# Loads that wait for an instruction instead of a copy, in an attention and expert kernel of one core

## The chip, the cores and the metric

The kernel runs on one core of a Trainium2 chip. The core has a matrix engine (TensorE, "PE" in the profile, with its weight loads shown apart as "PEld"), a vector engine (VectorE, "DVE"), a scalar engine (ScalarE, "ACT"), a general engine (GpSimd, "POOL") and an engine that mostly issues transfers (SyncE, "SP"). Each engine works through its own instructions in order and waits on semaphores for the others; 16 DMA engines move data between the memory outside (HBM) and the one on the core (SBUF). Sums of matrix products are collected in a third memory, PSUM, which has eight banks of 512 numbers per partition.

The metric is device time in microseconds for one execution. Two kernels are compared by the median of several runs of each.

## What is computed

An attention over 8 batches, 8 heads, 576 positions and 64 numbers per head, whose scores get a bias that falls with a running sum of `s`, and behind it a layer of 8 experts, where each token either picks its own expert or keeps that of the token before it:

```python
scores = scale * q @ k.T                                  # causal
cum = cumsum(maximum(s, 0))
attn = softmax(scores - (cum[query] - cum[key]))
x = attn @ v                                              # (8, 576, 512)
logits = x @ w_gate
e = argmax(logits) if s == 0 or sigmoid(x @ w_local) < 0.5 else previous e
out = softmax(logits)[e] * (relu(x @ w1[e]) @ w2[e])
```

Everything is in 32-bit floats. The bias is not added to the scores: the kernel multiplies each value row by exp(cum) of its key ("weighing"), and divides at the end by the sum of the same weights, which it gets from an extra column.

## The kernel before

The order of the instructions on every engine is written out by hand: an engine runs its instructions in the order in which the program names them. A tile of SBUF or PSUM comes from a pool with a fixed number of buffers; whoever first writes a reused buffer waits until its earlier readers are done.

**The attention** works on 32 pairs of heads (four pairs per batch), two pairs in each of 16 *slots*; `m` counts slots, `n` pairs. In a slot TensorE first makes the scores of the slot's two pairs in three units each (`scores`, L903 to L923, matmuls at L916), then half blocks of the diagonal (`scores_halves`, L938, for the next slot, and `values_halves`, L987, for this one), then the weighted sums of the first pair, "po", and of the second, "pb" (`values`, L975). ScalarE turns each unit of scores into exponentials (tile `e`, L917), GpSimd masks the diagonal (L900), VectorE divides (`evacuate`, reciprocal into `recs` and multiply, L997). Scores and the pairs' "pb" sums share three double banks of PSUM in turn (`banks`).

**The weighing** (`weigh`, L885 to L893): a copy on ScalarE (L890) writes the weights' column and two multiplications on VectorE (L893) write the value rows, all into one of four `vg` tiles. It needs the table `wk` of key weights, which is made once, in slot 0: exponentials of the running sum on ScalarE (L857, L858), seven transposes on TensorE (L866) and nine copies on VectorE (L872). `WEIGHED` gives the last pair weighed by the end of each slot.

**The loads** of keys (`kb`), queries (`qb`) and values (`va`) are issued by SP, in order: 288 KB for `kb` and `qb`, 320 KB for `va`. The first four pairs' loads stand at the start. Pair 0's queries and keys come in two parts each so that the first scores can begin early (L807). Later loads are spread over the slots. A slot has named places: `e00` to `e21`, behind each exponential (first digit the unit, second the pair of the slot), `h` behind the half blocks, `x0`, `x1` behind the first pair's two divisions, `y0`, `y1` behind the second's; `POINTS` says which places a slot uses, and `parts_of` gives the loads in order. To keep a load from starting before its place, the program writes one element of the target tile with a copy on ScalarE from something made at that place (L815 for values, L1064 for queries and keys, L548 for weights), so that the load has to wait for the copy:

```python
nc.scalar.copy(to[0:1, 0:1], behind)
nc.sync.dma_start(to, (q, k)["qk".index(what)][b][:, hp])
```

**Other work of the slots** is put at numbered places by `plan(slot, place, f)`: places 0 and 1 behind the two pairs' scores, 3 and 4 behind the first and second pair's divisions, 5 at the end. Among it are the router's products (L222, `lp`), its ranks (L307, L308), and scatters of the result into a table in HBM by GpSimd (L355), most of them in slots 7 to 15. Four loads of 512 KB each, the quarters of the first expert's first weights, are at place 3 of slots 11, 12, 13 and 13.

**The experts** (`Experts.run`) follow: 23 units of tokens, first layer (L614, L605), ReLU on ScalarE (L616), second layer (L643), a scatter to the output (L647). The second weights of the first expert are loaded behind the first ReLU of unit 0, with such a copy (L548); the router's last product also stands in unit 0.

Of the kernel before, what the change touches and what calls it, by code (L numbers as in the profile page):

```python
# [48 lines left out]
XW = 4 * 32 + 2  # L49
NV = 4  # L50
NVA = 6
WEIGHED = (3, 7, 9, 11, 11, 13, 15, 19, 19, 21, 23, 27, 27, 30, 31, 31)
STORES = (((5,), (0, 1, 3, 4, 5), (0, 1, 3, 4, 5), (0, 1, 3, 4, 5), (0, 0)), ((5, 5), (0, 1, 3, 4, 5), (0, 1, 3, 4, 5), (0, 1, 1, 3, 4, 5)),
          ((5, 5), (0, 0, 1, 1, 3, 4, 5, 5)))
BX = 3
FIRST = 3 * P
POINTS = {0: ("h", "x0", "x1", "y0"), 1: ("e00", "e10", "e20", "e01", "e11", "h", "x0", "x1"), 2: ("e00", "e20", "e11", "h", "x0", "x1")}
CAP = N + DH
ROWS = E * CAP + 2 * P
EMPTY = 1 << 20  # L60
# [10 lines left out]
@with_exitstack  # L71
def kernel(
    ctx: ExitStack,
    tc: tile.TileContext,
    q: bass.AP,
    k: bass.AP,
    v: bass.AP,
    s: bass.AP,
    w_gate: bass.AP,
    w_local: bass.AP,  # L80
    wx: bass.AP,
    w1: bass.AP,
    w2: bass.AP,
    out: bass.AP,
):
    nc = tc.nc
    table = nc.dram_tensor("table", (ROWS, 4, XW), F32, kind="Internal")

    ctx.enter_context(tc.manual_schedule(engines=None))
    const = ctx.enter_context(tc.tile_pool(name="const", bufs=1))  # L90
    ident = const.tile([P, P], F32, name="ident")
    make_identity(nc, ident)
    recs = const.tile([P, NPAIR, NJ, 2], F32, name="recs")
    wend = const.tile([P, NPAIR * NJ], F32, name="wend")
    out_of = const.tile([P, 1], I32, name="out_of")

    with ExitStack() as main:
        router = Router(main, tc, ident, table)
        experts = Experts(main, tc, w1, w2, out, table, router)
        with ExitStack() as early:  # L100
            attention(early, tc, q, k, v, s, wx, ident, recs, wend, router, experts)
        experts.run(recs, wend, out_of)

    wrong = nc.values_load(out_of[0:1, 0:1], min_val=0, max_val=1 << 23,
                           skip_runtime_bounds_check_because="a count of elements and rows")
    with tc.If(wrong > 0):
        cum_d = nc.dram_tensor("cum", (B * H, S), F32, kind="Internal")
        x_d = nc.dram_tensor("x_tokens", (N, D), F32, kind="Internal")
        with tc.tile_pool(name="g_const", bufs=1) as g:
            lg = g.tile([P, NM, E + 1], F32, name="lg")  # L110
            nc.vector.memset(lg, 0.0)
            ebi = g.tile([P, NBLK], I32, name="ebi")
            idx_g = g.tile([P, NBLK], I32, name="idx_g")
            idx_s = g.tile([P, NBLK], I32, name="idx_s")
            gate = g.tile([P, NBLK], F32, name="gate")
            attention_general(tc, q, k, v, s, w_gate, w_local, cum_d, x_d, ident, lg)
            route(tc, ident, lg, ebi, idx_g, idx_s, gate)
            experts_general(tc, w1, w2, out, x_d, ident, ebi, idx_g, idx_s, gate)


class Router:
# [362 lines left out]
class Experts:  # L484
# [47 lines left out]
    def load(self, l, layer=None, part=None, behind=None):  # L532
# [7 lines left out]
        for i, src in enumerate((self.w1, self.w2)):  # L540
# [3 lines left out]
            if not part:  # L544
                pool = getattr(self, self.place(l))
                ws[i] = pool.tile([P, FK, D] if i else [P, DK, F], F32, name=f"w{i + 1}b")
                if behind is not None:
                    self.nc.scalar.copy(ws[i][0:1, 0, 0:1], behind)  # L548
            n = ws[i].shape[1] // parts
            c = slice((part or 0) * n, (part or 0) * n + n)  # L550
            self.nc.sync.dma_start(ws[i][:, c].rearrange("p c f -> p (c f)"),
                                   src[bass.ds(self.e, 1), :, c].rearrange("o p c f -> (o p) (c f)"))

    def fetch(self, u):
        if u >= len(self.units):
# [38 lines left out]
    def layer1(self, u, c):  # L594
# [18 lines left out]
        for k in range(DK):  # L613
            mm(ps[:, :w], lhsT=self.ws[ls[0]][0][:, k, c * P : c * P + P], rhs=xT[:, k, :w],  # L614
               start=(k == 0), stop=(k == DK - 1))
        nc.scalar.activation(self.hT[u][:, c, :w], ps[:, :w], Act.Relu)  # L616

    def turn_h(self, u):
        if self.units[u][0] not in "MT":
# [35 lines left out]
    def run(self, recs, wend, out_of):  # L655
# [14 lines left out]
        def late_rows():  # L670
# [4 lines left out]
            self.puts += router.pads()  # L675

        todo = {
            (0, 0): [lambda: self.load(0, 1, behind=self.hT[0][0:1, 0, 0:1]), lambda: self.load(1), lambda: router.assign_early(1), lambda: self.load(2)],
            (0, 2): [lambda: router.product(last, self.xts_of, self.banks, (1,)),
                     lambda: router.logits(last, (1,)), lambda: router.codes(last), lambda: router.exps(last),  # L680
                     lambda: router.turn1(last), lambda: router.turn2(last)],
# [90 lines left out]
def attention(ctx, tc, q, k, v, s, wx, ident, recs, wend, router, experts):  # L772
# [18 lines left out]
    def banks(name):  # L791
        return ps_s.tile([P, 2, 512], F32, name=name, tag="s")

    ins, vs, es, eh, xs, xts = {}, {}, {}, {}, {}, {}
    heads = [slice(DH * h, DH * h + DH) for h in range(2)]

    def load_qk(n, behind=None):

        if n >= NPAIR:
            return  # L800
        b, hp = divmod(n, HP)
        ins[n] = qb, kb = p_in.tile([P, S], F32, name="qb"), p_in.tile([P, S], F32, name="kb")
        if behind is not None:
            nc.scalar.copy(kb[0:1, 0:1], behind)
        todo = [(kb, k, 0, S), (qb, q, 0, S)] if n else [(kb, k, 0, DH + P), (qb, q, 0, FIRST), (qb, q, FIRST, S), (kb, k, DH + P, S)]
        for to, src, a, z in todo:
            nc.sync.dma_start(to[:, a:z], src[b][:, hp, a:z])  # L807

    def load_v(n, behind=None):
        if n >= NPAIR:  # L810
            return
        b, hp = divmod(n, HP)
        va = vs[n] = p_v.tile([P, NB, 2, DH], F32, name="va")
        if behind is not None:
            nc.scalar.copy(va[0:1, 0, 0, 0:1], behind)  # L815
        nc.sync.dma_start(va.rearrange("p c h d -> p (c h d)"), v[b, hp].rearrange("p c h d -> p (c h d)"))

    scratch = p_x.tile([P, NJ, 2, XW], F32, name="xb").rearrange("p c g f -> p (c g f)")
    s_sb, ones, cum = (scratch[: B * H, i * S : i * S + S] for i in range(3))
# [1 line left out]
    load_qk(0)  # L821
    for h in range(2):
        nc.scalar.dma_start(s_sb[h * NPAIR : h * NPAIR + NPAIR], s.rearrange("(n h) t -> h n t", h=2)[h])

    nc.vector.memset(zero, 0.0)
    nc.vector.memset(ones, 1.0)
# [5 lines left out]
    load_qk(3)  # L832
    load_v(2)
    load_v(3)
    router.projection(wx)
    wk = once.tile([P, NPAIR, G1 + NB, 2], F32, name="wk")
    nc.gpsimd.memset(wk[TL:, :, G1 + NF], 0.0)
    for t in vgs:
# [21 lines left out]
    def key_weights():  # L860
        cps = banks("cps")[:, 0].rearrange("p (i n) -> p i n", n=B * H)
        i = 0
        for w, n in ((w1, G1), (w2, NB)):
            for c in range(n):
                a = min(c * P, S - P)
                tr(cps[:, i], w[:, a : a + P], ident[: B * H, : B * H])  # L866
                i += 1
        for i in range(G1 + NB):
            d = slice(0, P)
            c = i - G1  # L870
            for to, of in (heads[:2],) if c == NF else (heads, heads[::-1]) if c in TURNED else ((d, d),):
                nc.vector.tensor_copy(wk[to, :, i, :].rearrange("p n h -> p h n"),  # L872
                                      cps[of, i].rearrange("p (h n) -> p h n", h=2))

    def range_ends():

# [26 lines left out]
    def scores(n, u):  # L903
# [8 lines left out]
        for c, a, z, at in UNITS[u]:  # L912
            key = 0 if c == NF else DH + c * P
            for a, z, at in ((a, FIRST, at), (FIRST, z, at + FIRST - a)) if (n, u) == (0, 0) else ((a, z, at),):
                for h, d in enumerate(heads):
                    mm(ps[:, h, at : at + z - a], lhsT=kb[d, key : key + P], rhs=qb[d, a:z], start=True, stop=True)  # L916
        nc.scalar.activation(e[:, :, : WIDTH[u]], ps, Act.Exp, scale=scale)  # L917
        if u == 0:
            masked(e[:, :, :DH], [[0, 2], [1, DH]], DH)
        elif u == 1:  # L920
# [70 lines left out]
    def evacuate(n, po, part):  # L991
        b, hp = divmod(n, HP)
        if b not in xs:
# [4 lines left out]
            xs[b][:, a:z, :, 32 * hp : 32 * hp + 32],  # L998
            po[part][:, :, :DH].rearrange("p j (g i) -> p j g i", g=2),
            rec[:, :, 0].unsqueeze(2).unsqueeze(3).to_broadcast([P, z - a, 2, 32]), op=Alu.mult)  # L1000
        for r in reads if n % 2 and not part else ():
            tc.add_to_no_dep_group(f"first{n}", r.ins)

# [38 lines left out]
            plan(i, p, lambda g=g, c=c, after=after: router.scatter(g, c, after))  # L1042
    m = NPAIR // 2
    plan(1, 5, router.constants)
    plan(2, 5, router.constants2)
    plan(2, 3, range_ends)
    plan(m - 5, 1, lambda: router.assign_early(0))
    for i in range(4):
        plan(m - 5 + min(i, 2), 3, lambda i=i: experts.load(0, 0, i))
    plan(m - 2, 0, lambda: (experts.fetch(0), experts.fetch(1)))  # L1050
    plan(m - 1, 0, lambda: experts.turn_x(0))
    plan(m - 1, 1, lambda: router.product(NG - 1, (xts[B - 2],), banks, (0,)))
# [6 lines left out]
    def qk_part(n, what):  # L1059
        def load(behind):  # L1060
            b, hp = divmod(n, HP)
            to = p_in.tile([P, S], F32, name=what + "b")
            ins.setdefault(n, [None, None])["qk".index(what)] = to
            nc.scalar.copy(to[0:1, 0:1], behind)  # L1064
            nc.sync.dma_start(to, (q, k)["qk".index(what)][b][:, hp])
        return load

    def v_part(n):
        return lambda behind: load_v(n, behind)

    def parts_of(m):

        vs_of = {0: (), 1: range(NV, NV + 4)}.get(m, range(2 * m + NV, 2 * m + NV + 2))
        return [v_part(n) for n in vs_of if n < NPAIR] + [
            qk_part(n, x) for n in (2 * m + NV, 2 * m + 1 + NV) if n < NPAIR for x in "kq"]

    parts, points = [], {}

    def let_go(place, behind):

        if parts and place in points:
            parts.pop(0)(behind)

    for m in range(NPAIR // 2):
        pair = 2 * m, 2 * m + 1
        parts = parts_of(m)
        points = POINTS.get(m, POINTS[2])
        for n in pair:
            for u in range(len(UNITS)):
                if (n, u) == (0, 1):  # L1090
# [3 lines left out]
                scores(n, u)  # L1094
                if (n, u) == (0, 2):
                    key_weights()
                    weigh(0)
                    weigh(1)
                let_go(f"e{u}{n % 2}", es[n][u][0:1, 0, P : P + 1])
            at(m, n - 2 * m)  # L1100
        a, b = pair
        po = room(a)
# [5 lines left out]
        to = room(b)  # L1108
        scores_halves(m + 1, halves)
        values_halves(b, to, True)  # L1110
        let_go("h", es[b][2][0:1, 0, P : P + 1])
        for i in range(2):
            if m:
                values(a, po, i, False, True)
            evacuate(a, po, i)
            let_go(f"x{i}", recs[0:1, a, PARTS[i][0], 0:1])
        at(m, 3)
        for i in range(2):
            values(b, to, i, False, True)
            evacuate(b, to, i)  # L1120
            let_go(f"y{i}", recs[0:1, b, PARTS[i][0], 0:1])
        assert not parts
        at(m, 4)
        last = m % HP == HP - 1
        if last:
# [587 lines left out]
```

## Time and profile before

| what | us |
|---|---|
| median of 8 runs | 747.62 |
| the eight runs | 747.14, 747.24, 747.37, 747.56, 747.69, 749.65, 750.3, 750.9 |
| the profiled execution, its own time | 750.18 |
| span of the profiled execution, first to last instruction | 748.5 |
| slots 0 to 15 in it | 0 to 224.1 |
| experts in it | 224.1 to the end |
| TensorE busy | 723.2 |
| ScalarE busy | 173.5 |
| VectorE busy | 251.8 |
| GpSimd busy | 203.6 |

The profile is one execution. It gives each engine's busy time, the groups of instructions by line, the waits (who stood, and whose semaphore came last), and the chain of work that ended last, followed back from the last instruction. "issue" in the chain or as a releaser is time in which the engine waited for nothing that the profile shows. The matmuls are pipelined and their ends are modelled, so that a busy TensorE may still be short of its best rate. Transfers are seen as packets on queues: q1 is SP's, q10 ScalarE's, q0 GpSimd's, and q8 and q14 carry blocks of instructions. The granted clock is TensorE's, 1.00 being full speed.

### The profile page before, as it was taken

What the parts mean: (1) busy time and instruction counts of PE and PEld (TensorE: products, weight loads), DVE (VectorE), ACT (ScalarE), POOL (GpSimd) and SP (SyncE); (2) the same over time, 40 slices, a digit from 0 to 9 for tenths busy, and PEclk for the clock granted to TensorE, in tenths of its full rate; (3) what the DMA queues carried; (4) which work ended last, traced back from release to release, by engine and by line L of the source; (5) the groups of instructions that cost most, each with busy time, mean ns of one, the idle gap of its engine ahead of it and who ended that gap; (6) DMA issues with size and microseconds to landing.
All of it is one profiled execution on the core that took longest, in us unless ns stands there. A gap on an engine that the chain in (4) does not pass through costs nothing.

```text
span 748.5 us, 17075 instructions
## 1 busy us (share of the span) xinstructions
PE 723.2 (97%) x6925; PEld 495.2 (66%) x6925; DVE 251.8 (34%) x689; ACT 173.5 (23%) x423; POOL 203.6 (27%) x421
## 2 busy tenths in 40 slices
PE   8999999999888999999999999999999999999996
PEld 7687867767767567567567365637644676673675
DVE  4556856666757383100100411051133001104110
ACT  4556555455421011011011010201010110110111
POOL 3452366666654345340100011010101001000100
PEclk9999999999999999999999999999999999999999
DMA  6664555666628997598555978996999965876700
GB/s 214 208 191 155 168 175 164 188 198 194 204 75 335 365 381 251 198 422 252 191 191 178 364 267 350 375 380 218 422 365 387 413 229 212 306 271 239 268 15 32
DMA packets 57207, 187.33 MB, mean 250 GB/s; under 512 B 11837, under 2 KB 32061, under 8 KB 49568
## 3 DMA queue, kind: packets, MB, share of 16 engines
q1 hardware_dynamic: 50224, 165.91, 63.2%
q0 software_dynamic: 6800, 20.09, 7.0%
q8 instruction: 56, 0.92, 0.5%
q14 instruction: 31, 0.25, 0.1%
q10 hardware_dynamic: 96, 0.15, 0.1%
HBM read 165.50 MB, written 20.75 MB: 249 GB/s over the span
## 4 chain that ended last, share of the span: by engine, by line
PE 95%; issue 2%; ACT 2%; DVE 0%; POOL 0%; POOLq 0%; ACTq 0%
PE yp L643 34%; PE hp L614 31%; PE ps L916 9%; PE pb L975 6%; PE po L975 6%; PE hp L605 4%; PE lp L222 2%; ACT e L917 1%; PE ph L938 1%; PE pb L987 1%; PE po L987 1%; PE warm L845 1%; DVE wk L872 0%; PE pos L307 0%; POOL e L900 0%
## 5 line engine op out<-in xcount | busy, mean ns | idle before, releaser
L643 PE MATMUL yp<-w2b,hT 128*128 128x512 f32 (+4 forms) x768 | 258.4, 584 | 0.0
L614 PE MATMUL hp<-xT,w1b 128*128 128x256 f32 (+2 forms) x1216 | 231.2, 351 | 0.0
L614 PEld LDWEIGHTS hp<-xT,w1b 128*128 128x128 f32 x1216 | 207.0, 191 | 30.0 <-issue 8.1
L643 PEld LDWEIGHTS yp<-w2b,hT 128*128 128x128 f32 (+3 forms) x768 | 109.9, 167 | 138.4 <-issue 136.1
L616 ACT ACTIVATE hT<-hp 128x256 f32<-128x256 f32 (+2 forms) x152 | 53.6, 352 | 429.5 <-PE hp L614 415.3
L647 POOL DMA_INDIRECT out_dram<-y,gi x37 | 36.4, 984 | 412.3 <-DVE y L645 373.9
L645 DVE TENSOR_SCALAR y<-yp,gi 128x512 f32<-128x512 f32 (+2 forms) x38 | 27.8, 731 | 295.2 <-PE yp L643 282.5
L917 ACT ACTIVATE e<-ps 128x1024 f32<-128x1024 f32 (+2 forms) x96 | 83.2, 905 | 45.4 <-PE ps L916 45.4
L916 PE MATMUL ps<-qb,kb 64*128 64x64 f32 (+5 forms) x644 | 82.9, 407 | 1.0 <-DMA qb<-in_q_dram 0.6
L916 PEld LDWEIGHTS ps<-qb,kb 64*128 64x128 f32 x644 | 52.4, 187 | 29.6 <-ACT e L917 9.8
L355 POOL DMA_INDIRECT table<-xb,idx x54 | 53.9, 998 | 17.8 <-issue 16.7
L900 POOL TENSOR_SCALAR_AFFINE_SELECT e<-e 128x128 f32<-128x128 f32 (+2 forms) x96 | 42.9, 452 | 52.5 <-ACT e L917 51.1
L975 PE MATMUL pb<-vg,e 128*64 128x66 f32 x1344 | 47.3, 223 | 7.8 <-issue 7.7
L625 DVE STREAM_TRANSPOSE hT<-hs 32x256 f32<-32x256 f32 x64 | 27.9, 436 | 78.9 <-ACT hs L607 78.1
L975 PEld LDWEIGHTS pb<-vg,e 128*64 128x64 f32 x1344 | 43.2, 138 | 10.6 <-issue 10.5
L975 PE MATMUL po<-vg,e 128*64 128x66 f32 x1344 | 45.0, 224 | 2.7 <-issue 2.7
L975 PEld LDWEIGHTS po<-vg,e 128*64 128x64 f32 x1344 | 41.6, 138 | 5.0 <-issue 3.9
L893 DVE TENSOR_TENSOR vg<-va,wk 128x256 f32<-128x256 f32 x64 | 38.5, 666 | 0.0
L584 DVE STREAM_TRANSPOSE xT<-xq 128x1024 f32<-128x1024 f32 (+1 forms) x23 | 23.6, 1028 | 15.1 <-DMA xq<-table 14.9
L605 PE MATMUL hp<-w1b,xT 128*32 128x512 f32 (+1 forms) x224 | 28.3, 594 | 0.0
L900 POOL TENSOR_SCALAR_AFFINE_SELECT eh<-eh 64x512 f32<-64x512 f32 (+1 forms) x32 | 21.3, 665 | 12.1 <-ACT qb L1064 7.9
L605 PEld LDWEIGHTS hp<-w1b,xT 128*32 128x32 f32 (+1 forms) x224 | 8.1, 114 | 17.8 <-issue 17.8
(273 smaller groups left out, 329.1 us busy)
## 6 DMA issues: line engine op xcount, KB each, us to landing
w2b<-in_w_dram SPq DMA_DIRECT2D x30, 2048.0 KB
w1b<-in_w_dram SPq DMA_DIRECT2D x29, 2048.0 KB
va<-in_v_dram SPq DMA_DIRECT2D x32, 320.0 KB
kb<-in_k_dram SPq DMA_DIRECT2D x31, 288.0 KB
qb<-in_q_dram SPq DMA_DIRECT2D x31, 288.0 KB
xq<-table SPq DMA_DIRECT2D x56, 130.0 KB
w1b<-in_w_dram SPq DMA_DIRECT2D x4, 512.0 KB
xq<-table SPq DMA_DIRECT2D x20, 65.0 KB
```

Source lines behind the costliest of these rows:

```text
L355: put = self.nc.gpsimd.indirect_dma_start(out=self.halves, in_=src, element_offset=0, in_offset=None, out_offset=bass.IndirectOffsetOnAxis ...
L605: mm(ps[d, :], lhsT=xT[:, k, d], rhs=self.ws[l][0][:, k, c * 512 : c * 512 + 512], start=(k == 0), stop=(k == DK - 1))
L614: mm(ps[:, :w], lhsT=self.ws[ls[0]][0][:, k, c * P : c * P + P], rhs=xT[:, k, :w], start=(k == 0), stop=(k == DK - 1))
L616: nc.scalar.activation(self.hT[u][:, c, :w], ps[:, :w], Act.Relu)
L625: self.nc.vector.transpose(hT[32 * a : 32 * a + 32, :, 32 * r : 32 * r + 32], hs[32 * r : 32 * r + 32].rearrange("p (c i) -> p c i", i=P)[ ...
L643: mm(ps[d, :], lhsT=hT[:, k, n * P + d.start : n * P + d.stop], rhs=self.ws[l][1][:, k, f : f + w], start=(k == 0), stop=(k == FK - 1))
L647: put = nc.gpsimd.indirect_dma_start(out=self.out[:, :], out_offset=bass.IndirectOffsetOnAxis(ap=gi.bitcast(I32)[:m, n, 0:1], axis=0), in_ ...
L893: nc.vector.tensor_tensor(vg[:, to].rearrange("p c h e -> p (c h) e")[:, :, :DH], va[:, :c].rearrange("p c h e -> p (c h) e"), wk[:, n, to ...
L900: nc.gpsimd.affine_select(out=ap, in_=ap, compare_op=Alu.is_ge, fill=0.0, base=base, pattern=n, channel_multiplier=-1)
L916: mm(ps[:, h, at : at + z - a], lhsT=kb[d, key : key + P], rhs=qb[d, a:z], start=True, stop=True)
L917: nc.scalar.activation(e[:, :, : WIDTH[u]], ps, Act.Exp, scale=scale)
L975: of = mm(po[part][d, j - a, :], lhsT=weights_of(n, c, j, h), rhs=vgs[n % NV][:, c if j < 2 * G1 else G1 + c, h, :], start=(first and i == ...
```

## The change

1. **No copies.** A new function `held` adds a semaphore wait to the transfer itself, on the instruction behind which it shall start: the exponential (kept in `exps`) or the reciprocal (kept in `recips`). The copies at L815, L1064 and L548 go. `POINTS` and `parts_of` become `transfers(m)`, which names the place of each load. Slots 2 to 15 keep their places. The value load of pair 4 moves into slot 0 (place `e11`), and slot 1's seven loads stand at `e00`, `e10`, `e20`, `e11`, `h`, `x0`, `x1`.
2. **Quarters.** The four quarters of the first weights wait for the last reciprocal (`y1`) of slots 11, 12, 13 and 14.
3. **First slot.** Pair 0's second part of the keys is split in two, and its second part of the queries goes to ScalarE's queue. The weighing of pairs 0 and 1, so far behind pair 0's scores, comes behind pair 1's second and third unit. The router's weights `wx` are loaded at the end of slot 1 instead of the start.
4. **Fewer copies of weights.** The nine copies into `wk` become four larger ones.
5. `WEIGHED` lets slot 1 weigh pairs 4 and 5 alone, and slot 2 pairs 6 to 9.

```diff
-WEIGHED = (3, 7, 9, 11, ...
+WEIGHED = (3, 5, 9, 11, ...
+def held(tc, dma, behind):
+    if behind is not None:
+        tc.add_manual_dep(dma.ins, behind.name, mybir.DependencyInfo(mybir.DependencyClass.Sync, mybir.DependencyReason.DATA),
+                          reason="a transfer's time")
...
-                if behind is not None:
-                    self.nc.scalar.copy(ws[i][0:1, 0, 0:1], behind)
-            self.nc.sync.dma_start(ws[i][:, c].rearrange("p c f -> p (c f)"),
-                                   src[bass.ds(self.e, 1), :, c].rearrange("o p c f -> (o p) (c f)"))
+            held(self.tc, self.nc.sync.dma_start(ws[i][:, c].rearrange("p c f -> p (c f)"),
+                                                 src[bass.ds(self.e, 1), :, c].rearrange("o p c f -> (o p) (c f)")), behind)
...
-        nc.scalar.activation(self.hT[u][:, c, :w], ps[:, :w], Act.Relu)
+        self.relu = nc.scalar.activation(self.hT[u][:, c, :w], ps[:, :w], Act.Relu).ins
...
-            (0, 0): [lambda: self.load(0, 1, behind=self.hT[0][0:1, 0, 0:1]), ...
+            (0, 0): [lambda: self.load(0, 1, behind=self.relu), ...
...
-        todo = [...] if n else [(kb, k, 0, DH + P), (qb, q, 0, FIRST), (qb, q, FIRST, S), (kb, k, DH + P, S)]
+        todo = [...] if n else [(kb, k, 0, DH + P), (qb, q, 0, FIRST), (kb, k, DH + P, DH + 2 * P), (kb, k, DH + 2 * P, S)]
...
+    nc.scalar.dma_start(ins[0][0][:, FIRST:], q[0][:, 0, FIRST:])
...
-    router.projection(wx)
+    plan(1, 5, lambda: router.projection(wx))
...
-        for i in range(G1 + NB):
-            d = slice(0, P)
-            c = i - G1
-            for to, of in (heads[:2],) if c == NF else (heads, heads[::-1]) if c in TURNED else ((d, d),):
-                nc.vector.tensor_copy(wk[to, :, i, :].rearrange("p n h -> p h n"),
-                                      cps[of, i].rearrange("p (h n) -> p h n", h=2))
+        i = G1 + TURNED[0]
+        for to, of, at in ((slice(0, P), slice(0, P), slice(0, i)), (*heads, slice(i, i + 2)), (*heads[::-1], slice(i, i + 2)),
+                           (*heads, slice(i + 2, i + 3))):
+            nc.vector.tensor_copy(wk[to, :, at, :].rearrange("p n i h -> p i h n"),
+                                  cps[of, at].rearrange("p i (h n) -> p i h n", h=2))
...
-    for i in range(4):
-        plan(m - 5 + min(i, 2), 3, lambda i=i: experts.load(0, 0, i))
...
-            nc.scalar.copy(to[0:1, 0:1], behind)
-            nc.sync.dma_start(to, (q, k)["qk".index(what)][b][:, hp])
+            held(tc, nc.sync.dma_start(to, (q, k)["qk".index(what)][b][:, hp]), behind)
...
+    def transfers(m):
+        n = 2 * m + NV
+        k0, q0, k1, q1 = (qk_part(n + i, x) for i in range(2) for x in "kq")
+        if m == 0:
+            return {"e11": v_part(4), "h": k0, "x0": q0, "x1": k1, "y0": q1}
+        if m == 1:
+            return {"e00": v_part(5), "e10": v_part(6), "e20": k0, "e11": q0, "h": k1, "x0": q1, "x1": v_part(7)}
+        of = {"e00": v_part(n), "e20": v_part(n + 1), "e11": k0, "h": q0, "x0": k1, "x1": q1} if n < NPAIR else {}
+        i = m - NPAIR // 2 + 5
+        if 0 <= i < 4:
+            of["y1"] = lambda behind: experts.load(0, 0, i, behind)
+        return of
...
-                    weigh(0)
-                    weigh(1)
-                let_go(f"e{u}{n % 2}", es[n][u][0:1, 0, P : P + 1])
+                if n == 1 and u:
+                    weigh(u - 1)
+                let_go(f"e{u}{n % 2}", exps[n, u])
```

## The prediction

> **What bounds the kernel now.** I read the page first. TensorE is busy for nearly the whole span and nearly the whole chain that ended last runs over it:
>
> ```profile
> span 748.5 us, 17075 instructions
> PE 723.2 (97%) x6925; PEld 495.2 (66%) x6925; DVE 251.8 (34%) x689; ACT 173.5 (23%) x423; POOL 203.6 (27%) x421
> PE 95%; issue 2%; ACT 2%; DVE 0%; POOL 0%; POOLq 0%; ACTq 0%
> ```
>
> The change touches no matmul, so it can win only TensorE's idle time, 748.5 - 723.2 = 25.3 us, and of that only what lies where the change works. Second, the busy times cut at the slots (a slot is one pair of head pairs; columns: stretch, its length, then busy time and count of each engine, clock, DMA share, GB/s):
>
> ```profile
> 0.00:19.61 19.61, 17.29 (x332) 14.88 (x332) 8.68 (x25) 9.35 (x19) 7.05 (x25) 1.00 0.64 214
> 19.61:33.28 13.67, 11.81 (x277) 9.54 (x273) 6.08 (x14) 7.12 (x18) 6.48 (x23) 1.00 0.79 253
> 33.28:44.70 11.42, 11.42 (x277) 9.31 (x274) 8.73 (x18) 6.73 (x15) 7.36 (x27) 1.00 0.50 152
> 150.60:164.40 13.80, 12.42 (x275) 9.80 (x274) 8.41 (x29) 6.77 (x16) 10.34 (x20) 1.00 0.70 205
> 208.50:224.10 15.60, 13.64 (x306) 10.72 (x305) 8.30 (x23) 4.96 (x6) 10.26 (x22) 1.00 0.16 56
> ```
>
> Slot 2 (third row) has no idle TensorE at all, though it still issues three load copies during its exponentials. Slot 0 is idle for 2.32 us and slot 1 for 1.86. Slots 11 and 15 (last rows) lose 1.38 and 1.96, slot 15 with a DMA share of only 0.16.
>
> Third, the chain in slots 0 to 2, where those idle times become waits:
>
> ```profile
> 11.04 0.32 ACT vg L890 x2
> 11.36 0.92 ACT e L917
> 12.32 0.92 PE ps L916 x8
> 13.25 2.60 PE po L975 x84
> ...
> 25.10 0.90 ACT e L917
> 26.05 0.46 PE pb L987 x16
> 26.51 2.60 PE po L975 x84
> ...
> 31.49 1.52 issue
> 33.01 0.33 PE pb L975 x3
> ...
> 39.27 0.43 PE pb L987 x16
> 39.71 2.60 PE po L975 x84
> ```
>
> In slot 0 the path leaves TensorE for VectorE's weight copies and ScalarE; in slot 1 it runs over the exponentials; then TensorE stands for 1.52 us with nothing that the trace names. Slot 2 shows the undisturbed timing.
>
> **The change, part by part.** The profiled execution took 750.18 us, its span 748.5, so 1.68 lies around it, which I leave alone.
>
> *Load copies.* 28 (L815) + 56 (L1064) + 1 (L548) = 85 copies of one element go, 0.19 us each by their rows, 16 us of ScalarE. ScalarE is idle for three quarters of the span, so this pays only where the exponentials set the path. That is slot 1. With a copy between, exponentials start 22.00 - 20.84 = 1.16 us apart; the slot-2 pair without one overlaps so that the second starts about 0.1 us before the first ends, 0.92 apart, so a copy costs 0.22 to 0.24. Four of them, 0.9 us. But TensorE takes over first: in slot 2 the line L987 begins 39.27 - 33.35 = 5.92 us after the slot's first scores; slot 1's began at 19.68, so it could begin at 25.60 instead of 26.05. Value: -0.45 (bounds 0, and -0.9 if TensorE could follow all the way). In every later slot the cover is TensorE's own 5.07 us of scores, which ScalarE matches; value 0 there.
> The waits move to SP's queue: a load now holds back the loads behind it until its exponential or reciprocal is done. SP was waiting for the copy of that same event, so each issue comes about 0.2 us sooner, never later. In the slots with the router's product the second load waited on ScalarE behind its copies of logits (issued at 118.09, while that exponential ended near 114); it goes 4 us earlier, into scores that hide it. Bounds -0.5 to +0.5, value 0.
>
> *Slot 0.* Nine copies of the key weights, 0.265 us each, became four: one of 128x256, two of 64x128, one of 64x64. No copy of those shapes ran; the nearest rows are 0.265 (128x64) and 0.41 (the 128x256 multiply at L893, its fastest), so the four take 1.1 to 1.6 us against 2.07, and wk is ready at about 10.2 instead of 10.96. ScalarE no longer stands 1.27 us for it ahead of pair 1's exponentials, because weighing comes behind them. What is late next is pair 1's query load: TensorE waited 0.61 us for it until 9.46. From there: 1.08 us of scores, exponential from 10.62 to 11.64, the remaining scores and the halves behind it until 12.8; the copy of vg follows the next exponential at about 12.65. So the sums of pair 0 begin near 12.83 instead of 13.25: -0.42. Against it stands the finer split: one more issue on ScalarE's queue (0.44 us like its two others, under an engine idle for 3.18 us) and 128 more packets in a phase whose DMA share is 0.96 to 1.0. Bounds: +0.6 if pair 1's load lands that much later, -1.2 if every wait of slot 0 but the 1.13 us before the first matmul went.
>
> *The 1.52 us.* The DMA view of two stretches tells what the chain can't (queue, packets, MB, share of 16 engines):
>
> ```profile
> q1 hardware_dynamic: 664, 1.47, 83.1%
> ...
> q1 hardware_dynamic: 335, 0.67, 58.9%
> q8 instruction: 1, 0.02, 1.9%
> ```
>
> The first line is the stretch 24.5 to 30.2, with no instruction block in it; the others are 30.2 to 33.4, where one block lands while TensorE stands. Slots 2 and 3 draw two blocks each and have no such idle time at DMA shares of 0.50 and 0.58. I read it as TensorE's next instructions coming late behind a full load queue. Between 18 and 32 us some 3,584 KB were moved. After the change v4 and k4 (608 KB) go at about 12.4 and 14.2, into the hole at 14 to 18 us where the share was 0.06; 17% less remains for that stretch, and each load starts 0.2 to 1.2 us sooner. Value: the whole 1.52, since a block that comes in time costs nothing. Bounds 0 and -1.52.
> [...] The trace's 1.52 us at an arriving block speaks for the row.
>
> *First weights' quarters.* Four loads of 512 KB go from place 3 of slots 11, 12, 13, 13 to the ends of slots 11 to 14. Do they cause TensorE's idle time there? Slots 7, 8, 9, which carry no quarters, lose 1.08, 1.57, 1.26; slots 11, 12, 13 lose 1.38, 1.56, 2.17. Slot 13 also has one more scatter. So scatters, not quarters, go with this idle time, as slot 15 shows with its quiet DMA. At most 0.3 + 0.9 = 1.2 us; the same 0.6 in the other direction if the quarter now moved into slot 15 hits its product. Value 0. The last quarter is issued at about 208.8 behind the fetches, which SP finished at 207.15; 512 KB take about 3 us at slot 14's 173 GB/s, and unit 0 needs them at 224.1, so 12 us cover it.
>
> *Pair weights and router weights.* Two of slot 1's four weighings go to slot 2's end: 2 x 1.2 us of VectorE, done about 2.4 us into slot 3, 2.6 us ahead of their use. The router's load waits no longer in the first queue but behind slot 1; its use is at 61.27. Value 0.
>
> Sum: -0.45 - 0.42 - 1.52 = -2.4. On the profiled execution that is 747.8. But of the eight runs five lie at 747.14 to 747.69 and three, like the profile, at 749.65 to 750.9. The profile shows something that could make this difference of 2.9 us:
>
> ```profile
> 231.00:234.00 3.00, 0.67 (x9) 0.49 (x12) 1.14 (x7) 0.00 (x0) 1.75 (x3) 0.98 1.02 427
> 234.00:237.30 3.30, 3.30 (x27) 2.58 (x26) 2.01 (x11) 0.00 (x0) 0.00 (x0) 0.50 1.05 442
> ```
>
> Router's product in unit 0 stands twice, 1.17 and 1.16 us, while weights stream at 427 GB/s, and then the granted clock is 0.50 for 3.3 us. Cost: 2.33 + 0.70 (21 matmuls in 1.22 us, not 0.52) + 1.34 (40 in 9.97, not 8.63) = 4.4. I infer, and can't show, that the five quick runs miss most of it. The change reaches it only by one copy less ahead of that weights' load (0.2 us): value 0, bounds -4.4 and +4.4. The three terms therefore apply to the median: 747.62 - 2.4 = 745.2.
> [...]
>
> **The rivals.** (a) The stall at 31.5 stays, or moves to the next full stretch: 747.62 - 0.9 = 746.7. For it: v7 is still issued at about 29 us, so the queue is full near 30; against it, the smaller backlog. (b) Slower: the 0.2 us earlier weights' load makes the product of unit 0 starve in most executions. It decides once the weights' first packets are there when that product begins, 229.7; they were issued at 227.17. Price between the groups' 2.9 and the full 4.4: 745.2 + 2.9 to 4.4 = 748.1 to 749.6. Against it: three of eight runs are already so with the old timing, and SP's second weights' load waits for other things. (c) More is won: the quarters' 1.2 us, and a share of the 12 us idle in slots 7 to 15, because loads beside scatters start sooner: 745.2 - 1.2 to 3 = 742.2 to 744. Against it: slot 15. (d) The load still waits for the same event, so the copies' removal does nothing outside slot 1: that is already in the forecast.
>
> **How the numbers follow.** Forecast 0.5 (its own range 744.3 to 746), (a) 0.17, (b) 0.11, (c) 0.22. The range 742.6 to 748.2 leaves out about half of (b) and a little of (c). About 0.3%, 2.24 us, is what a measurement of this kernel can tell from no change: faster means below 745.38. The forecast's middle lies just beyond it, so 0.6 of its share, 0.30, and all of (c), 0.22, are faster; the rest of it, (a) and nearly all of (b) are the same, 0.42; slower 0.06, where (b) meets a failing term.
>
> **What would show it.** Right: slot 1's L987 about 5.92 us after its first scores; no long issue piece in slot 1 and a block of instructions ahead of 30 us; wk in four pieces, and pair 0's sums near 12.8. Slots 7 to 15 keep their short issue pieces. Wrong: a wait of TensorE for DMA in slot 0 or 2, idle time in slots 11 to 13 falling by more than 1 us, or a clock of 0.50 after unit 0's product in executions that lacked it.

## The result, and the profile after

The changed kernel takes 745.22 us (median of 15 runs, 743.46 to 747.91). The kernel before, run beside it, takes 748.95 (42 runs, 746.66 to 752.01). The ratio is 0.9952, its 95% interval 0.9940 to 0.9965: 0.5% faster, about 3.6 us. The forecast was 745.2. Its gain, 2.4 us, counted from the 747.62 of the first eight runs, was a third too small; 42 runs put the kernel before 1.3 us higher, and the two errors cancel. That the two times agree this closely is luck.

The page of the profiled execution of the changed kernel, its span and busy times:

```profile
span 743.2 us, 16900 instructions
PE 719.3 (97%) x6925; PEld 495.7 (67%) x6925; DVE 253.0 (34%) x684; ACT 160.8 (22%) x338; POOL 204.0 (27%) x421
PE 96%; issue 2%; DMA 1%; ACT 0%; POOL 0%; POOLq 0%; DVE 0%
```

85 instructions of ScalarE are gone (423 to 338). TensorE runs the same 6,925 matmuls but is *busy* 3.9 us less. The prediction took busy time as fixed ("it can win only TensorE's idle time"); this line says that it isn't. Of the 3.9 us, 2.6 lie in slots 2 to 15; 1.7 lie in the experts, where the kernel before had a stretch at half clock, and slots 0 and 1 together give 0.4 back.

The busy times of the changed kernel cut at slots 0, 1, 2 and 15 (columns as in the prediction):

```profile
0.00:21.07 21.07, 18.14 (x332) 15.45 (x332) 8.31 (x20) 8.89 (x15) 7.59 (x25) 1.00 0.78 247
21.07:32.57 11.50, 11.33 (x277) 9.42 (x273) 6.08 (x14) 5.65 (x9) 6.49 (x23) 1.00 0.65 204
32.57:43.67 11.10, 11.10 (x275) 9.29 (x272) 6.08 (x14) 5.86 (x10) 6.50 (x29) 1.00 0.57 178
204.96:220.58 15.62, 13.68 (x307) 10.80 (x305) 8.29 (x23) 4.96 (x6) 10.27 (x22) 1.00 0.26 89
```

Slot 1 fell from 13.67 to 11.50. Slot 2, which had no idle time to give, still fell from 11.42 to 11.10. Slot 15, which has no load of keys, queries or values, stayed. Slot 0 grew from 19.61 to 21.07. Over the whole span: slot 0 +1.46, slot 1 -2.17, slots 2 to 15 -2.81, experts -1.70; sum -5.2, this pair of executions being further apart than the medians.

The chain of waits in slots 0 to 2 of the changed kernel (start, length, what):

```profile
16.64 1.21 issue
...
21.14 4.96 PE ps L914 x40
...
26.96 0.23 PE pb L985 x16
...
32.64 4.96 PE ps L914 x40
...
38.46 0.23 PE pb L985 x16
38.69 2.60 PE po L973 x84
```

In slot 1 the path stays on TensorE, and the half blocks begin 26.96 - 21.14 = 5.82 us after the first scores (5.92 was forecast). The issue piece of 1.52 us is gone, but one of 1.21 us stands in slot 0. Slot 2 holds the surprise: scores take 4.96 us where the kernel before had 5.07, and the 16 half blocks 0.23 where it had 0.43. The line of the kernel before, just ahead of its two for slot 2 in the prediction:

```profile
33.35 5.07 PE ps L916 x40
```

From first scores to first sums that is 38.69 - 32.64 = 6.05 us; before, it was 39.71 - 33.35 = 6.36. The profile shows TensorE without idle time in both, and yet 0.31 us went.

### The profile page after: what moved, and what is told of

Same layout as the page of the kernel before. It is cut to its first block, busy times and chain, and to the rows that moved or that the text cites. A ratio compares the mean times of both kernels' runs of the same rounds, so it can differ in the third digit from the quotient of the medians.

```text
span 743.2 us, 16900 instructions
## 1 busy us (share of the span) xinstructions
PE 719.3 (97%) x6925; PEld 495.7 (67%) x6925; DVE 253.0 (34%) x684; ACT 160.8 (22%) x338; POOL 204.0 (27%) x421
## 4 chain that ended last, share of the span: by engine, by line
PE 96%; issue 2%; DMA 1%; ACT 0%; POOL 0%; POOLq 0%; DVE 0%
PE yp L647 34%; PE hp L618 31%; PE ps L914 10%; PE pb L973 6%; PE po L973 6%; PE hp L609 4%; PE lp L228 2%; PE ph L936 1%; PE po L985 1%; PE pb L985 1%; DMA qb<-in_q_dram 1%; DMA xb<-in_s_dram 0%; PE pos L313 0%; PE pos L314 0%; ACT e L915 0%
## 5 line engine op out<-in xcount | busy, mean ns | idle before, releaser
L915 ACT ACTIVATE e<-ps 128x1024 f32<-128x1024 f32 (+2 forms) x96 | 79.9, 931 | 68.2 <-PE ps L914 68.0
L914 PEld LDWEIGHTS ps<-qb,kb 64*128 64x128 f32 x644 | 54.2, 189 | 26.8 <-issue 8.0
```

Source lines behind the costliest of these rows:

```text
L915: exps[n, u] = nc.scalar.activation(e[:, :, : WIDTH[u]], ps, Act.Exp, scale=scale).ins
```

## The experiments

They ran on three chips, and each kernel is compared with the kernel before on its own chip: about 748 us on one (e5 to e8), 725.7 and 725.1 on the others (e1 to e4; e9 to e12). Those 23 us lie mostly in slots 7 to 15, where TensorE stood for 0.3 to 0.5 us again and again on the first chip and did not on the others, and some 3 us at unit 0's product. Times of one slot are from the profiles. "Busy" is TensorE's busy time by the view of stretches, taken over slots 2 to 15.

### Are the copies worth 0.3 us in every slot?

**e1** puts the 84 copies for keys, queries and values back, at the changed places:

```diff
-        held(tc, nc.sync.dma_start(va.rearrange("p c h d -> p (c h d)"), ...), behind)
+        if behind is not None:
+            nc.scalar.copy(va[0:1, 0, 0, 0:1], behind)
+        nc.sync.dma_start(va.rearrange("p c h d -> p (c h d)"), ...)
...
-                let_go(f"e{u}{n % 2}", exps[n, u])
+                let_go(f"e{u}{n % 2}", es[n][u][0:1, 0, P : P + 1])
```

> The changed kernel with the 84 one-element copies on ScalarE put back ahead of the loads of keys, queries and values, at the changed kernel's places; all else as changed. Theory A: the copies delay the exponentials in every slot, and TensorE's modelled ends hide the wait; a slot without stalls goes from 11.11 us back to 11.41, and the time is 3.5 to 4.5 us above the changed kernel's, a ratio to before of about 1.000. Rival B, the prediction's: copies cost 0.45 us in slot 1 and nothing in slots 2 to 15; clean slots stay at 11.11, the time is within 0.6 us of the changed kernel's, ratio about 0.996.

**e2** is the kernel before with the waits in place of the copies, and nothing else of the change:

```diff
-            nc.scalar.copy(va[0:1, 0, 0, 0:1], behind)
-        nc.sync.dma_start(va.rearrange("p c h d -> p (c h d)"), ...)
+        held(tc, nc.sync.dma_start(va.rearrange("p c h d -> p (c h d)"), ...), behind)
```

> The kernel before with its 85 copies replaced by waits of the transfers on the same exponentials and reciprocals; nothing else of the change. Theory A: clean slots at 11.11 us, slot 1 shorter by 0.45, about 4.5 us less in all, ratio about 0.994; the 1.52 us stall in slot 1 stays, as its loads stay. Rival B: 0.5 us less, ratio about 0.9993, clean slots at 11.41.

**e4** is the changed kernel once more, on the same chip.

> The changed kernel itself, as the yardstick of these runs: ratio 0.994 to 0.9965, slot 0 about 21 us with a stall of about 1.2 us in its half blocks if that stall belongs to the kernel, 19.8 if it was an accident of one execution; clean slots 11.11.

Slot 2 in the chain of e1:

```profile
31.86 5.07 PE ps L916 x40
...
37.79 0.43 PE pb L987 x16
38.22 2.60 PE po L975 x84
```

The old 6.36 us are back, to the hundredth, with every other part of the change in place. Slots 2 and 5 take 11.41 in e1 and 11.10 to 11.11 in e2 and e4. Busy time over slots 2 to 15:

| kernel | busy | idle |
|---|---|---|
| before; e5 (before again) | 178.73; 179.23 | 12.09; 11.74 |
| after; e6 (changed again); e8 | 176.12; 175.50; 176.03 | 11.89; 10.82; 12.24 |
| e1, copies back | 170.55 | 2.37 |
| e4; e9 (changed again); e3 | 167.61; 167.37; 167.75 | 4.10; 4.05; 5.61 |
| e2, before without copies (3.4 us of it at half clock) | 168.88 | 4.84 |

In both groups of chips the copies cost the same busy time: 179.0 - 175.9 = 3.1 us in the first two rows, 170.55 - 167.6 = 3.0 in the next two. So the mechanism of Theory A of e1 stands, clean slots of 11.41 and 11.11 us included, and its rival falls; of the 3.5 to 4.5 us of time that it named, 1.5 came, as the medians below show. The timeline shows what a copy does on ScalarE (start, length, engine, line, operation): four lines of the kernel before, then the six exponentials of slot 2 in the changed kernel.

```profile
34.51 1.02 ACT L917 ACTIVATE e<-ps 128x1024 f32<-128x1024 f32 x1 [0.91 <-PE ps L916]
35.57 0.19 ACT L815 COPY va<-e 1x1 f32<-1x1 f32 x1
35.67 1.59 ACT L917 ACTIVATE e<-ps 128x896 f32<-128x896 f32 x2
...
36.62 1.60 PEld L916 LDWEIGHTS ps<-qb,kb 64*128 64x128 f32 x16 [0.67 <-ACT e L917]
```

```profile
33.80 4.96 ACT L915 ACTIVATE e<-ps 128x1024 f32<-128x1024 f32 x6 [5.85 <-PE ps L914]
```

The exponential ends at 35.53; the next begins at 35.67, 0.14 us later, 1.16 us after its own predecessor began. In the changed kernel such a pair begins 0.92 apart. Three copies in a slot's exponentials make the last ones late (the sixth begins 4.81 us behind the first, in the changed kernel 4.11), and TensorE then waits for them in the middle of its matmuls (its weight loads of slot 2's scores stand 0.67 us for exponentials, the last line of the first view, and 0.44 in the changed kernel): 0.11 us in the scores, 0.20 at the half blocks. The profile counts this as busy time, presumably because a matmul's modelled end covers the wait. Only the start-to-start times, as the chain has them, show it.

The medians on that chip: e1 725.69 (ratio to before 0.9999, 0.9984 to 1.0013), e2 725.32 (1.0004, 0.9990 to 1.0018), e4 724.17 (0.9980, 0.9968 to 0.9992). So in time the copies cost 1.5 us between e1 and e4, whose intervals just overlap, and nothing that can be told between the kernel before and e2; e2 missed the 0.994 of its Theory A, and e4 the 0.994 to 0.9965 that was expected of it. e2 has the short slots and still isn't faster. Its profile suggests where it was given back: four long stalls of 0.9 to 2.0 us, and behind the longest one 3.4 us at half clock. That leads to the late blocks.

### First slot

**e3** gives pair 0's second part of the queries back to SP, and halves the keys' second part no longer:

```diff
-        todo = [...] if n else [(kb, k, 0, DH + P), (qb, q, 0, FIRST), (kb, k, DH + P, DH + 2 * P), (kb, k, DH + 2 * P, S)]
+        todo = [...] if n else [(kb, k, 0, DH + P), (qb, q, 0, FIRST), (qb, q, FIRST, S), (kb, k, DH + P, S)]
...
-    nc.scalar.dma_start(ins[0][0][:, FIRST:], q[0][:, 0, FIRST:])
```

> The changed kernel with pair 0's second part of queries back on SP's queue, ahead of the keys' second part, which is one transfer again; the late weighing and the four copies stay. Theory A: the part on ScalarE's queue landed late and put the first exponential at 6.96 us instead of 6.19; it comes back to about 6.2, pair 0's sums begin near 12.5 instead of 13.25, and slot 0 is 0.7 us shorter; ratio about 0.9943. Rival B: the queue doesn't matter, the first exponential is late by the order of bytes; it stays near 7.0 and the ratio at 0.9952.

724.64 (0.9985, 0.9972 to 0.9998), not to be told from e4. Its first exponential begins at 6.12 us, which looked like the answer to the 6.96 of the changed kernel's profile. But the changed kernel's three other executions (e4, e6, e9) have 6.33, 6.09 and 6.00, and the kernel before had 6.19 and, in e5, 6.74. So the begin of the first exponential varies from one execution to the next, here by up to 0.96 us; the finer split isn't the cause, and Theory A of this run falls. Slot 0 of e4 took 19.61 us, near the 19.8 that was expected if the stall of 1.2 us is an accident of one execution.

What hardly varies is the time from the first exponential to pair 0's first sums: 6.98 or 6.99 us in the kernel before, in e2 and in e5, 6.29 in ten of the eleven profiles with the late weighing and the four copies (6.49 in e8). These two parts together are worth 0.70; they weren't tried apart.

### Late blocks of instructions

The queue q8 brings blocks of instructions of 16 KB, 56 of them (0.92 MB) in the kernel before, up to the experts one per 129 matmuls (36 for 4,647); the author takes them for TensorE's. In all profiles taken, 44 stalls of TensorE between slot 0's half blocks and slot 15's end last over 0.5 us. Each of the 44 ends 1.24 to 1.55 us after such a block has landed (1.34 in the kernel before, 1.34 to 1.53 for the four of the changed kernel's profile), at the same few places of the program (the 218th matmul, the 600th, the 1106th, the 2249th, and so on), though not in every execution. Some 36 blocks land ahead of the experts in each execution, and at most five of them cost such a stall.

The stalls go with the change. In slots 2 to 15 each of the ten profiles without the copies (e11, which follows, apart) has three or four stalls over 0.5 us, 2.7 to 5.9 us together; the three with copies have none (before), none (e5) and two, 1.5 us together (e1).

**e11** doesn't load the last 16 pairs; their tiles are those of earlier pairs, so the kernel leaves out half of the attention's loads. Scatters and quarters stay:

```diff
+        if n >= 16:
+            vs[n] = kept[n - NVA * ((n - 10) // NVA)]
+            return
...
+            if n >= 16:
+                ins.setdefault(n, [None, None])["qk".index(what)] = ins[n - 4]["qk".index(what)]
+                return
```

> The changed kernel without the loads of queries, keys and values of pairs 16 to 31, whose sums use the tiles of earlier pairs again; the scatters, the first weights' quarters and all matmuls stay. Theory I: long stalls, in which TensorE goes on about 1.4 us after a block of instructions has landed, come from loads ahead of that block; none is left in slots 7 to 10, while the short stalls beside scatters stay. Rival J: scatters alone make blocks late; the long stalls stay, and slots 7 to 13 keep their idle time.

Beside it ran e9, the changed kernel:

> The changed kernel, as the yardstick of these four runs: clean slots 11.11 us, 6.29 us from the first exponential to pair 0's first sums, and long stalls wherever a block of instructions lands late.

e11 takes 719.15 us, e9 723.47, one run each.

TensorE's waits in e11 for nothing that the profile shows, all of them (total, times, longest, in us):

```profile
PE pb L978 <- issue: 0.4, 1, 0.4
PE ph L941 <- issue: 0.4, 1, 0.4
...
PE po L978 <- issue: 0.3, 1, 0.3
```

Three waits in all: two lie in slots 0 and 1, where loads still run, one in slot 15. Slots 6 to 14 have none at all, where the ten other profiles without copies have two or three over 0.5 us each, and the idle time of slots 2 to 15 is 0.46 us where e9 has 4.05. So the loads make the blocks late, as Theory I has it, and Rival J, that scatters alone do, falls. Whether a block stands behind the loads or beside them isn't shown, and the short stalls beside scatters, which Theory I expected to stay, hardly occur on this chip.

**e12** puts the load of pair 4's values back into slot 1:

```diff
-            return {"e11": v_part(4), "h": k0, ...
+            return {"h": k0, ...
...
-            return {"e00": v_part(5), "e10": v_part(6), "e20": k0, "e11": q0, "h": k1, "x0": q1, "x1": v_part(7)}
+            return {"e00": v_part(4), "e10": v_part(5), "e20": v_part(6), "e01": v_part(7), "e11": k0, "h": q0, "x0": k1, "x1": q1}
```

> The changed kernel with the first two slots' loads at the places of the kernel before: pair 4's values in slot 1, which then has eight loads. The prediction: slot 1 gets a stall of 1.5 us back, and slot 0's half blocks lose the stall of 0.65 to 1.2 us that four of the changed kernel's executions show. Rival K: the places move the stall between the two slots by chance; slots 0 and 1 together change by less than 0.5 us and the time by less than 0.6.

The chain at the end of its slot 1:

```profile
30.60 1.53 issue
```

The old stall is back, at the old place, with the old length (1.52), and the one in slot 0 is gone: its half blocks run from 16.31 without a pause. The other profiles agree. With the loads at the old places (before, e2, e5, e12) slot 0's half blocks never stall, and slot 1's end stalls 1.52, 0.93, 0 and 1.53 us; at the new places slot 0's half blocks stall 0.39 to 1.21 us in eight of ten profiles (not in e8 and e10), and slot 1's end at most 0.71. So the places decide which block tends to be late; e12 moves other loads of slot 1 too, so that pair 4's values alone do it is not shown. The time is 724.80 (0.9993, 0.9975 to 1.0010), 1.3 us more than the one run of e9 on the same chip.

But the stall isn't a fixed part of the kernel before. **e5** is that kernel again, and **e6** the changed one beside it:

> The kernel before, for its profile on the chip of these runs. Theory A: clean slots 11.41 us, as in the first profile, whatever the chip; slot 1 has its stall of about 1.5 us behind a late instruction block, and TensorE takes up again about 1.4 us after that block has landed. Rival C, that stalls are accidents of one execution: slot 1 is clean apart from 0.45 us.

> The changed kernel, for its profile on the same chip. Theory A: clean slots 11.11 us; the 14 slots behind slot 1 win 14 x 0.3 = 4.2 us less what late blocks give back, so slots 2 to 15 are 0 to 4.2 us shorter than in the kernel before on this chip. Rival B: clean slots differ by nothing.

e5 takes 747.23, and its slot 1 loses 0.31 us, not 1.86. e6 takes 743.43. Their slots add up: slot 0 20.02 to 19.38 (-0.64), slot 1 11.88 to 11.77 (-0.11), slots 2 to 15 190.97 to 186.32 (-4.65, a little beyond Theory A's 4.2), experts 522.64 to 524.24 (+1.60, a stretch at half clock); together -3.8. In e6 the blocks were late elsewhere: 0.39 us in slot 0, 0.45 in slot 1, 0.64 in slot 3, 1.47 in slot 7, 0.82 in slot 11.

### Unit 0's product

**e7** issues the weights' loads of unit 0 behind its fourth ReLU, so that the router's product has the transfers to itself:

```diff
-            (0, 0): [lambda: self.load(0, 1, behind=self.relu), lambda: self.load(1), lambda: router.assign_early(1), lambda: self.load(2)],
+            (0, 0): [lambda: router.assign_early(1)],
+            (0, 3): [lambda: self.load(0, 1, behind=self.relu), lambda: self.load(1), lambda: self.load(2)],
```

> The changed kernel with unit 0's weight loads (its second weights and those of the next two) held behind the fourth ReLU instead of the first, so that they start behind the router's last product. Theory D: the stream of weights starves that product (1.17 and 1.16 us in the profile before); without it the product takes its 1.6 to 2.4 us, the long stalls go, the clock never halves there, and the time is 2 to 4 us below the changed kernel's where it has that stall, equal where it has not. Rival E: the scatters beside it starve it; nothing changes, or the later weights make the second layer of unit 0 wait for DMA and the kernel is 1 to 5 us slower.

749.84, 0.2% slower than before (1.0019, 1.0004 to 1.0035) and 6.4 us above e6. Two lines of its waits:

```profile
PE yp L647 <- DMA w2b<-in_w_dram: 4.2, 1, 4.2
PE lp L228 <- issue: 2.6, 5, 1.1
```

The product stalls as before (3.0 us in e6, 2.6 here), though no load moved on SP's queue between 225.6 and 229.6 us and the DMA share was 0.28, and the second layer now waits 4.2 us for its weights. Theory D, that the weights' load starves the product, falls; the cost is the one that Theory E named. What those five waits of the product are for stays open.

### Quarters and scatters

**e8** puts the four quarters back to place 3 of slots 11, 12, 13, 13; **e10** moves the scatters of places 3 and 4 of six slots to place 5:

```diff
+    for i in range(4):
+        plan(m - 5 + min(i, 2), 3, lambda i=i: experts.load(0, 0, i))
...
-        if 0 <= i < 4:
-            of["y1"] = lambda behind: experts.load(0, 0, i, behind)
```

```diff
-STORES = (((5,), (0, 1, 3, 4, 5), (0, 1, 3, 4, 5), (0, 1, 3, 4, 5), ...
+STORES = (((5,), (0, 1, 5, 5, 5), (0, 1, 5, 5, 5), (0, 1, 5, 5, 5), ...
```

> The changed kernel with the four quarters of the first weights back at place 3 of slots 11, 12, 13, 13, without a wait. The prediction: their place is worth nothing, slots 11 to 14 keep their length within 0.5 us and the time within 0.6 us of the changed kernel's. Rival F: beside the second pair's sums they make instruction blocks late; slots 11 to 13 grow by 1 to 1.5 us each time a block is hit.

> The changed kernel with the scatters at places 3 and 4 of slots 7 to 9 and 11 to 13 moved to place 5, so that GpSimd issues them during the next slot's scores. Theory G: the short stalls of 0.35 to 0.4 us in the second pair's sums belong to a scatter beside many small matmuls; the sums of those slots lose their short stalls, 0.5 to 1 us in each of six slots, 3 to 6 us in all on a chip that shows them, a ratio to before of 0.988 to 0.992 there. Rival H: the three scatters in a row hold up GpSimd's masks of the next slot, TensorE waits for masks, and the kernel is 1 to 6 us slower than the changed one.

e8 takes 743.61 (0.9948, 0.9929 to 0.9966), e6 beside it 743.43 in its one run. Slots 11 to 14 take 13.55, 15.87, 14.66 and 12.51, in e6 13.52, 15.79, 14.64 and 11.96: 0.7 us in sum, a little more than the 0.5 expected and most of it in slot 14, and 0.2 in the time, where the seven runs of e8 spread over 3.2. The quarters' move is worth nothing that these runs can tell. e10 takes 726.37 (1.0006, 0.9988 to 1.0024). It ran on a chip without the short pauses that it was to test, so Theory G stays open; the waits for masks of Theory H don't show. Its profile shows late blocks instead, the longest 2.56 us in slot 7.

## Why the prediction was right, and where it wasn't

The total was right; two of its terms were not, in opposite directions, and that they nearly cancelled is luck.

**Copies: the step that failed.** "In every later slot the cover is TensorE's own 5.07 us of scores, which ScalarE matches; value 0 there." The 5.07 us themselves held a wait of 0.11 for the copies, and 0.20 more stood at the half blocks. e1 and the table of busy times give 3.0 to 3.1 us of busy time for slots 2 to 15, the largest part of the gain; late blocks gave part of it back, so that the time fell by 1.5 us from e1 to e4. The cover was read from a busy time that contained the cost. The 0.45 us forecast for slot 1 is of the right kind, but undisturbed slot 1 fell from 11.88 (e5) to 11.50 to 11.77. Rival (d), that nothing happens outside slot 1, falls with it.

**The 1.52 us: right mechanism, wrong as a sum.** That loads make a block late, and that the places of the first slots' loads decide which one, is what e11 (0.46 us idle in slots 2 to 15, 4.05 in e9) and e12 (1.53 us at slot 1's end again) show. But "the whole 1.52" took one execution's stall for a fixed cost: e5 doesn't have it, so a median holds less of it. In the profiled execution after the change the same block landed at 30.8 us, not ahead of 30, and cost 0.17. At the new places another block is late, in slot 0 (1.21 us in the profiled execution, 0.39 in e6 and e4, 0.66 in e1). Rival (a), that the stall moves, is nearer to what happened. The count here is none to five long stalls for some 36 blocks ahead of the experts, and each cost 0.53 to 2.56 us.

**Slot 0: mis-sized.** -0.42 was forecast for the later weighing and the four copies; the interval they act on fell by 0.70; yet pair 0's sums began at 13.25 us in the profiled execution, not at 12.83, because its first exponential came at 6.96 instead of 6.19. The four copies took 1.68 us, just above the forecast's 1.1 to 1.6 us, and no longer lie on the path. The slot as a whole gained 0.64 from e5 to e6 and lost 1.46 from before to after, as its first exponential came 0.77 us later and a block was late (1.21 us).

**Quarters, router's weights, pair weights: 0.** e8 bears this out for the quarters; the others weren't tried alone.

**Half clock at unit 0's product: forecast at 0.** Before and e6 have it, after and e5 don't, with the old and the new load. So the change doesn't govern it, and rival (b) didn't come; how often each kernel has it wasn't counted. The 1.70 us that the experts gained from before to after go with it, as do the 1.60 that they lost from e5 to e6, and are no gain of the change.

**The balance.** Where the kernel takes about 748 us, the idle time of slots 2 to 15 stayed at 11 to 12 us: long stalls came (none before and in e5, 2.7 to 3.2 us after and in e6, e7 and e8), and pauses of 0.2 to 0.5 us went (27 and 26 of them, 10.1 and 9.5 us; then 20 to 22, 7.0 to 8.0). So the 3 us of busy time are left there; with 0.7 for slot 0 and 0.1 to 0.4 for slot 1, less 0.4 to 1.2 for the block in slot 0, that is near the 3.6 measured. On the two quicker chips there were hardly any short pauses to lose, and the gain is smaller: 1.5 us with e4, 1.6 with e9. From e1 to e4 busy time fell by 2.9 while idle time rose by 1.7. That slots 2 to 15 lose more to long stalls without the copies holds for every profile compared; whether the shorter slots or the earlier loads do it wasn't tried. No kernel tried that does all the work beats the changed one by more than its spread.

## What to carry to other kernels

A load that has to start behind an instruction should wait for that instruction itself; a one-element copy in a row of exponentials costs 0.24 us of ScalarE each here, and may reach TensorE though the profile shows TensorE busy. Busy time won is not yet time won: here about half of it came back as idle time behind late instruction blocks (e1 to e4), and in e2 nothing of it could be told in the median. Before an edit is costed at nothing because an engine is "busy", compare start-to-start times of the same group between a slot with the suspect and one without it. And a stall that one execution shows at an instruction block should enter a sum only with the share of executions that have it: take a second profile first.

## What the hardware showed

**Half clock behind idle gaps.** Two lines of e6, the stretches around unit 0's product, and one of the changed kernel's profile behind the same product (TensorE's clock is the third number from the end):

```profile
224.00:227.04 3.04, 0.68 (x9) 0.35 (x4) 1.42 (x9) 0.00 (x0) 2.08 (x3) 0.97 0.96 377
227.04:230.45 3.41, 3.41 (x25) 2.73 (x25) 1.99 (x11) 0.00 (x0) 0.00 (x0) 0.52 1.04 437
```

```profile
230.20:234.00 3.80, 3.80 (x35) 3.27 (x35) 2.77 (x14) 0.00 (x0) 0.00 (x0) 1.00 0.99 416
```

Gaps of 1.15 and 1.14 us with two matmuls between them were followed by 3.4 us at half clock in e6, and so were those of 1.17 and 1.16 in the kernel before; gaps of 1.14 and 1.10 in the changed kernel's profile were not. A single stall of 2.02 us (e2) or 2.56 (e10) was followed by it too, one of 1.89 (e8) was not. So the sum of the gaps alone doesn't tell: 2.24 us in the changed kernel cost no clock, 2.02 in e2 did. In the kernel before, the trace's record of the granted clock has a slow stretch of 3.413 us, which begins 228.69 us after the first moment at full speed, 67 times its own length. Counted off in this length from that moment, both gaps of the kernel before lie in one stretch, the one just ahead of the slow one, with 2.49 us idle, as those of e6 do, with 2.21; the changed kernel's lie in two, with 1.32 and 1.10. That this is what parts them is the author's estimate from these three profiles; no run tried it.

**Chips differ.** The same kernel takes 748 us on one chip and 725 on two others, each tried at one time only, nearly all of it in pauses and longer busy times of slots 7 to 15, where GpSimd scatters. In slots 2 to 15 e4 and e9 lose 4.1 us of idle time, after and e6 11 to 12, and TensorE is busy 8 us longer. What makes the pauses wasn't found.
